# An FFT block with an ELU feed-forward layer on one core: prologue reordered, x rows moved to partition 0, scratch tensors padded, A units of batch 1 placed ahead of most Y units

## The chip, the cores and the metric

The kernel runs on one core of one Trainium2 chip. The metric is the device time of the whole program in microseconds (us). Besides the times there is one profiled execution with a trace of every instruction; its engines are named PE (matmuls), PEld (weight loads of PE), DVE, ACT, POOL and SP, and a trailing q (ACTq, SPq) marks an engine's issuing of DMAs. Times in the trace count from the start of the span.

## The reference, cut to what matters

```python
# x: (8, 3008, 256); w_r, w_i: (256, 256); w_in: (256, 2048); w_out: (2048, 256)
X = np.fft.rfft(x, axis=1)
Yr = Xr @ w_r - Xi @ w_i + b_r
Yi = Xr @ w_i + Xi @ w_r + b_i
Yr = np.sign(Yr) * np.maximum(np.abs(Yr) - 0.01, 0.0)      # Yi the same
y = np.fft.irfft(Yr + 1j * Yi, n=3008, axis=1)
h = y.reshape(-1, 256) @ w_in
g = np.where(h > 0.0, h, np.exp(np.minimum(h, 0.0)) - 1.0)
out = g @ w_out
```

A real FFT over the sequence, a complex linear layer with soft shrinkage, the inverse FFT, then a feed-forward layer of width 2048 with an ELU.

## The kernel before

The sequence of 3008 is split as 47 x 64 (N1 x N2), and both transforms are done as matmuls with matrices of sines that the kernel computes itself at its start. For each of the eight batches there are five kinds of units:

- **A** (`unit_A`, eight units per batch, two per chunk `ci` of x): the first step of the forward transform. Two f32 matmuls take a chunk of x from the tile `xts[ci]` with the matrix M1; the result is evicted to the tile A and stored in the scratch tensor DA in DRAM.
- **X** (`unit_X`, six): DA is read back in another order into the tile Z (`load_Z`), and eight matmuls with M2 give the spectrum XT.
- **M** (`unit_M`, twelve): the complex linear layer with bias and shrinkage (PE, then DVE, then two POOL operations).
- **B** (`unit_B`, six): the first step of the inverse transform with M3; the eviction goes to Bz and the result into the scratch tensor DB in DRAM.
- **Y** (`unit_Y`, eight): DB is read back as the tiles Bs (`load_Bs`, four), and matmuls with M4 give yT, the input of the feed-forward layer.

The feed-forward layer of a batch is a loop over 48 pairs (`PER`: six blocks of 512 tokens, eight pairs of feature tiles each). Each pair has a `front` (four matmuls, L582, then one or two ACT operations), an ELU on DVE and partly POOL (L602, L606, L617, L619; its result is gT) and, two pairs later, a `back` (eight matmuls, L639). `psH` has two buffers for what `front` writes, so that the front of pair i + 2 waits until the ELU of pair i has read its buffer. The units of the next batch are woven into this loop: `plan(b)` writes out for each pair which units run ahead of its front (`f0`) and which loads are issued behind it (`f1`). The single buffer of the pool `psF` serves one unit at a time. While batch 0 is in the feed-forward loop, `seq` begins with fourteen units: Y units 2 to 7 of batch 0, which is not yet fully transformed back, mixed with A units 0 to 7 of batch 1 (written "a"); after a7 the loads of Z of batch 1 are issued, and X unit 0 of batch 1 stands at pair 15. Behind them comes the list `mid`, which all batches share. It holds the six B units; at units 1, 3 and 5 the store of Bz to DB is issued from ACT (L246).

Batch 0 itself is transformed before the loop, in the **prologue**, with nothing to run beside it. Its parts in program order: 20 filler matmuls (`idle_pe`, on constant data, their result is not used); the loads of x, issued from POOL (`load_x`), each chunk as 80 + 14 rows that go to partitions 17 to 110 (P0 = 17) of tiles with 111 partitions; the zeroing of partitions 0 to 16, on ACT for chunks 0 and 1 (`zero_rows`, L314), on POOL for chunks 2 and 3 (L327); M1 from iotas and a sine; `phases(g)` on DVE (L385 to L394) and `sines(g, c)` on ACT (L401) for the three column groups g of M2; the A units with `alone=True`, whose stores are issued from SP (L133); the loads of Z; the transposes that give M4 and M3 (L451, L466); conversions of the weights (L474 to L477); the loads of the feed-forward weights; then X, M and B units of batch 0 and the stores of DB from SP (L241); the four loads of Bs, half from SP and half from ACT; filler matmuls while they come; Y units 0 and 1. A small POOL copy (`gate`) holds POOL until a given tile has landed, so that the x loads of batch 1 are issued only behind the first Bs.

Each engine executes its own instructions in program order, and the order is written by hand throughout. A DMA is issued by the engine named in the code and stands in that engine's order.

Of the kernel before, what the change touches and what calls it, by code (L numbers as in the profile page):

```python
# [8 lines left out]
ALU = mybir.AluOpType  # L9
# [12 lines left out]
NH = N2 // 2  # L22
P0 = N2 - N1
P1 = P0 + 2 * N1


@with_exitstack
def kernel(
# [66 lines left out]
    def load_x(b, ci):  # L95
        xv = x[b].rearrange("(r m c) d -> c r m d", c=4, m=8)
        for r0, r1 in ((0, 80), (80, 2 * N1)):
            nc.gpsimd.dma_start(xts[ci][P0 + r0 : P0 + r1], xv[ci, r0:r1].bitcast(F32R))

# [11 lines left out]
    def unit_A(b, u, alone=False, on_dve=False):  # L111
        ci, uu = u // 2, u % 2
        if uu == 0:
            if alone:
                A_of[b, ci] = wk4.tile([4 * K1, 8, D], BF16, name="A", tag="Bs")
            else:
                A_of[b, ci] = wk2.tile([4 * K1, 8, D], BF16, name="A", tag="A")
            if ci == 0:
                DA_of[b] = dram.tile([NH, 4 * K1, D], BF16, name="DA", tag="DA")
        xt, A = xts[ci], A_of[b, ci]  # L120
        dav = DA_of[b].rearrange("(m c) r d -> c r m d", c=4)
        ps = unit_ps("aps", alone)
        for j in range(2):
            nc.tensor.matmul(  # L124
                ps[0 : 4 * K1, j, :], lhsT=M1[:],
                rhs=xt[:, 4 * uu + 2 * j : 4 * uu + 2 * j + 2, :], start=True, stop=True,
            )
        evac(
            A[:, 4 * uu : 4 * uu + 4, :].rearrange("p n d -> p (n d)"),
            ps[0 : 4 * K1].rearrange("p a b -> p (a b)"), on_dve,  # L130
        )
        if alone:
            nc.sync.dma_start(dav[ci, :, 4 * uu : 4 * uu + 4, :], A[:, 4 * uu : 4 * uu + 4, :])  # L133
        elif uu == 1:
            nc.scalar.dma_start(dav[ci], A[:])
# [79 lines left out]
    def unit_B(b, v, alone=False, on_dve=False):  # L215
        if v % 2 == 0:
            Bz_of[b, v // 2] = wk2.tile([P, 8, D], BF16, name="Bz", tag="Bz")
            if v == 0:
                DB_of[b] = dram.tile([K1, P, D], BF16, name="DB", tag="DB")
        Bz, Y = Bz_of[b, v // 2], Y_of.pop((b, v))  # L220
        ps = unit_ps("bps", alone)
        for pp in range(2):
            for c in range(2):
                for s in range(2):
                    nc.tensor.matmul(  # L225
                        ps[:, s, pp * D : pp * D + D],
                        lhsT=M3[s * N2 : s * N2 + N2, 2 * v + pp, c, :],
                        rhs=Y[s * N2 : s * N2 + N2, pp, c * D : c * D + D],
                        start=(c == 0), stop=(c == 1),
                    )  # L230
        o = 4 * (v % 2)
        Bv = Bz[:, o : o + 4, :].rearrange("p (q s) d -> p s q d", s=2)
        psv = ps[:].rearrange("p s (q d) -> p s q d", d=D)
        if on_dve:
            nc.scalar.copy(Bv[:, 0], psv[:, 0])
            nc.vector.tensor_copy(Bv[:, 1], psv[:, 1])
        else:
            nc.scalar.copy(Bv, psv)  # L238
        if alone:
            k0 = 4 * v  # L240
            nc.sync.dma_start(  # L241
                DB_of[b][k0 : k0 + 4].rearrange("k p d -> p k d"), Bz[:, o : o + 4, :]
            )
        elif v % 2:
            k0 = 8 * (v // 2)
            nc.scalar.dma_start(DB_of[b][k0 : k0 + 8].rearrange("k p d -> p k d"), Bz[:])  # L246

    def load_Bs(b, w, engs=None):
        engs = engs or (nc.sync, nc.sync)
        Bs = wk4.tile([4 * K1, 8, D], BF16, name="Bs", tag="Bs")  # L250
        dv = DB_of[b].rearrange("k (c m) d -> (k c) m d", c=2)
        for h in range(2):
            n0 = h * NH + 8 * w
            engs[h].dma_start(Bs[h * 2 * K1 : h * 2 * K1 + 2 * K1], dv[:, n0 : n0 + 8, :])
        Bs_of[b, w] = Bs
# [32 lines left out]
    with tc.tile_pool(name="stagep", bufs=1) as stagep:  # L288
# [22 lines left out]

        def zero_rows(ci):
            for m in range(0, 8, 2):
                nc.scalar.activation(  # L314
                    xts[ci][0:P0, m : m + 2, :].rearrange("p n d -> p (n d)"), busy[0:P0, :],
                    AF.Copy, scale=0.0,
                )

        pcol = iota([P, 1], "pcol", [[0, 1]], cm=1)
# [4 lines left out]
        for ci in range(1, 4):  # L324
            load_x(0, ci)
        for ci in range(2, 4):
            nc.gpsimd.memset(xts[ci][0:P0].bitcast(F32), 0.0)  # L327
        ident = stagep.tile([P, P], F32, name="ident")
# [6 lines left out]
        def wrap(v, r):  # L335
# [4 lines left out]

        half = col("half", pcol, 0.5, ALU.mult, -0.5 * P0 - 0.25, ALU.add)
        halfm = col("halfm", half, CMAGIC, ALU.add)
# [7 lines left out]
        wrap(v1[:], r1t[:])  # L350
        zero_rows(0)
        nc.scalar.activation(r1t[:], v1[:], AF.Sin, bias=0.0, scale=SIN_SCALE)
        zero_rows(1)
        h1col = stagep.tile([P, 1], F32, name="h1col")
        nc.vector.scalar_tensor_tensor(
            h1col[:], n1col[:], -2.0, pcol[:], ALU.mult, ALU.add
        )
        h1col = col("h1m", h1col, float(-P0), ALU.add)
        isx = col("isx", pcol, P0 - 0.5, ALU.is_gt)
        h0col = stagep.tile([P, 1], F32, name="h0col")  # L360
        nc.vector.scalar_tensor_tensor(
            h0col[:], h1col[:], -1.0, isx[:], ALU.mult, ALU.add
        )
        nc.vector.tensor_tensor(h0col[:], h0col[:], isx[:], ALU.mult)
        nc.vector.tensor_tensor(h1col[:], h1col[:], isx[:], ALU.mult)
        ccol = col("ccol", pcol, N2 - 0.5, ALU.is_gt)
# [38 lines left out]

        for g in range(2):
            phases(g)
# [23 lines left out]
        unit_A(0, 3, alone=True)  # L431
        sines(1, 0)
        idle_pe(4)
        unit_A(0, 4, alone=True)
# [4 lines left out]
        unit_A(0, 6, alone=True)  # L439
        unit_A(0, 7, alone=True, on_dve=True)  # L440
        phases(2)
        sines(1, 1)
        dume = stagep.tile([P, 1], F32, name="dume")
        sines(2, 0)
        sines(2, 1)
        nc.scalar.activation(dume[:], pcol[:], AF.Exp, scale=0.0)
        for g in range(3):
            load_Z(0, 8 * g, 8 * g + 8, 0, NH, (nc.sync, nc.scalar))

# [5 lines left out]
        nc.vector.tensor_scalar(  # L455
            M4[:], m4ps[0 : 4 * K1, P0:P1], wcol[0 : 4 * K1, :], None, ALU.mult
        )
# [3 lines left out]
        for g in range(3):  # L461
# [8 lines left out]
            nc.vector.tensor_copy(M3[:, 4 * g : 4 * g + 4, :, :], m3ps[:])  # L470
            if g == 1:
                idle_pe(6)
        idle_pe(10)
        nc.vector.tensor_copy(wcat_r[:, :, 0:D], w_r_f[:])  # L474
# [68 lines left out]
    for q in range(4):  # L543
        nc.vector.tensor_scalar_mul(
            w_in_s[:, :, q * FQ : q * FQ + FQ], w_in_f[q][:], 2.0 / S
        )
    idle_pe(28)
    for u in range(2):
# [122 lines left out]
    def plan(b):  # L671
# [11 lines left out]
        if b == 0:  # L683
            lead, seq = 1, (
                [("y", 2), ("a", 0), ("a", 1), ("y", 3), ("a", 2), ("a", 3), ("y", 4), ("a", 4),
                 ("a", 5), ("y", 5), ("a", 6), ("a", 7), ("y", 6), ("y", 7)] + mid
            )
# [91 lines left out]
```

## Time and profile before

| what | value |
|---|---|
| median of 3 runs | 968.77 us (967.47 to 969.27) |
| profiled execution, whole time | 967.99 us |
| its span, from first to last instruction | 966.2 us |
| PE busy | 924.5 us |
| PE busy from 60.6 to 180 us | 111.72 of 119.40 us |
| PE busy from 295 to 410 us | 113.44 of 115.00 us |
| ACT busy from 295 to 410 us | 90.75 of 115.00 us |
| DB store issued from ACT (L246) | 21 times, 382 ns each |
| DB store issued from SP (L241) | 6 times, 360 ns each |
| DA store issued from ACT (L135) | 28 times, 328 ns each |

The share of busy time is an average over the prologue (some 60 us), the stretch in which batch 0 and batch 1 overlap (60 to 180 us), and six more stretches of about 115 us each, in the last of which nothing but the feed-forward layer is left. The page also shows the span in 40 equal slices:

```profile
PE   6969899999999999999999999999999999999997
PEclk9879999999999999999999999999999999999999
DMA  9996941856165543836246461665438102411011
```

Each digit is a slice of 24.2 us: the busy share in tenths for PE, the granted clock of PE in tenths, the busy share of the DMA engines. Slices 1 and 3 are the prologue's beginning and the stretch from 48 to 72 us.

### The profile page before, as it was taken

The page shows a single profiled execution, that of the slowest core. Times are in us where ns is not written, and L with a number is a line of the kernel's source. Part 1 is how long each engine was busy: PE and PEld are TensorE (multiplying, and loading weights), DVE is VectorE, ACT ScalarE, POOL GpSimd, SP SyncE. Part 2 cuts the span into 40 slices and gives each one's busy share as a digit, 9 for nine tenths or more (in the row PEclk, how much of TensorE's full clock was granted, in tenths as well). Part 3 has the DMA queues.
Part 4 walks back from the last instruction along what each step waited for, and adds up shares of the span by engine and source line. Part 5 has one row for each costly group of instructions (what it writes and reads, how often), then busy time and mean ns, then how long its engine had stood idle before and what let it go on. Part 6 is the DMA issues. An engine that isn't in the chain of part 4 may idle for free.

```text
span 966.2 us, 16677 instructions
## 1 busy us (share of the span) xinstructions
PE 924.5 (96%) x6398; PEld 655.5 (68%) x6502; DVE 733.9 (76%) x855; ACT 721.6 (75%) x819; POOL 281.1 (29%) x356
## 2 busy tenths in 40 slices
PE   6969899999999999999999999999999999999997
PEld 2436666777667766777667776776767777677775
DVE  8747666776788777887778777787778867888996
ACT  6538678888877788778886888877887787667664
POOL 5520343034302442115312243024421143321332
PEclk9879999999999999999999999999999999999999
DMA  9996941856165543836246461665438102411011
GB/s 215 271 191 109 185 90 45 217 107 129 45 185 128 87 76 83 220 56 115 71 133 161 74 119 55 179 136 87 76 82 212 33 22 66 110 45 42 22 44 42
DMA packets 113987, 105.43 MB, mean 109 GB/s; under 512 B 7794, under 2 KB 107636, under 8 KB 113012
## 3 DMA queue, kind: packets, MB, share of 16 engines
q1 hardware_dynamic: 41892, 54.02, 21.1%
q0 software_dynamic: 27680, 26.74, 19.8%
q10 hardware_dynamic: 44336, 23.60, 9.4%
q8 instruction: 51, 0.84, 0.4%
q14 instruction: 28, 0.23, 0.1%
HBM read 54.53 MB, written 49.81 MB: 108 GB/s over the span
## 4 chain that ended last, share of the span: by engine, by line
PE 57%; DVE 20%; ACT 12%; issue 4%; DMA 4%; POOL 1%; ACTq 1%; DVEq 0%; SPq 0%; another core or an unknown queue 0%; POOLq 0%
PE ps_o L639 21%; PE hps L582 21%; DVE gT L602 9%; PE mps L177 7%; DVE gT L606 4%; DVE Et L617 4%; ACT Et L592 3%; PE aps L124 2%; DVE Et L619 2%; ACT Et L589 2%; ACT A L109 2%; PE bps L225 2%; DMA xt<-in_x_dram 2%; PE xps L158 2%; ACT osb L651 2%
## 5 line engine op out<-in xcount | busy, mean ns | idle before, releaser
L639 PE MATMUL ps_o<-w_out_r,gT 128*128 128x256 f32 (+1 forms) x3072 | 491.9, 302 | 1.6 <-DVE gT L602 1.0
L639 PEld LDWEIGHTS ps_o<-w_out_r,gT 128*128 128x128 f32 (+1 forms) x3072 | 410.7, 187 | 67.6 <-DVE gT L602 12.9
L582 PE MATMUL hps<-yT,w_in_s 128*128 128x512 bf16 (+1 forms) x1465 | 386.4, 378 | 11.9 <-DVE gT L606 4.4
L592 ACT ACTIVATE Et<-hps 128x1024 f32<-128x1024 f32 (+1 forms) x300 | 302.0, 1007 | 102.1 <-PE hps L582 73.9
L602 DVE SCALAR_TENSOR_TENSOR gT<-Et,hps 128x1024 fp32r<-128x1024 f32 (+1 forms) x181 | 214.7, 1186 | 68.1 <-ACT Et L590 50.4
L606 DVE SCALAR_TENSOR_TENSOR gT<-hps,Et 128x1024 fp32r<-128x1024 f32 (+1 forms) x203 | 245.6, 1210 | 17.5 <-PE hps L582 0.5
L582 PEld LDWEIGHTS <-w_in_s 128*128 128x128 bf16 x1536 | 133.4, 98 | 152.2 <-issue 35.8
L619 DVE TENSOR_SCALAR Et<-Et 128x1024 f32<-128x1024 f32 (+1 forms) x203 | 139.0, 685 | 91.7 <-ACT Et L592 89.7
L192 POOL TENSOR_SCALAR clip<-yb 128x512 f32<-128x512 f32 x84 | 51.6, 614 | 313.1 <-DVE yb L184 258.8
L617 POOL TENSOR_SCALAR Et<-Et 128x512 f32<-128x512 f32 (+1 forms) x97 | 59.5, 613 | 274.3 <-ACT Et L592 274.3
L589 ACT ACTIVATE Et<-hps 128x1024 f32<-128x1024 f32 x84 | 86.4, 1029 | 69.9 <-PE hps L582 69.9
L193 POOL TENSOR_TENSOR Y<-yb,clip 128x512 bf16<-128x512 f32 x84 | 107.2, 1277 | 7.0
L184 DVE TENSOR_TENSOR yb<-mps,bias_bc 128x512 f32<-128x512 f32 x96 | 66.2, 690 | 32.9 <-PE mps L177 22.4
L590 ACT ACTIVATE Et<-Et 128x1024 f32<-128x1024 f32 x84 | 88.8, 1057 | 2.7
L109 ACT CAST A<-aps 96x1024 bf16<-96x1024 f32 x63 | 63.4, 1009 | 15.4 <-PE aps L124 14.9
L109 ACT CAST yT<-yps 128x752 bf16<-128x752 f32 x63 | 49.7, 788 | 18.8 <-PE yps L265 18.8
L177 PE MATMUL mps<-wcat_r,XT 128*128 128x512 bf16 x176 | 54.7, 384 | 0.6 <-ACT XT L165 0.2
L177 PE MATMUL mps<-wcat_s,XT 128*128 128x512 bf16 x177 | 53.9, 379 | 0.8
L617 DVE TENSOR_SCALAR Et<-Et 128x512 f32<-128x512 f32 (+1 forms) x97 | 54.2, 559 | 0.4 <-ACT Et L592 0.2
L168 ACT CAST XT<-xps 128x1024 bf16<-128x1024 f32 x46 | 45.9, 1000 | 10.4 <-PE xps L158 10.4
L177 PEld LDWEIGHTS <-XT 128*128 128x128 bf16 x384 | 30.7, 98 | 29.0 <-issue 1.1
L238 ACT CAST Bz<-bps 128x1024 bf16<-128x1024 f32 x47 | 47.3, 1008 | 3.6 <-PE bps L225 3.6
(95 smaller groups left out, 420.1 us busy)
## 6 DMA issues: line engine op xcount, KB each, us to landing
xt<-in_x_dram POOLq DMA_DIRECT2D x32, 640.0 KB, 6.2
out_dram<-osb SPq DMA_DIRECT2D x160, 128.0 KB
Bs<-DB SPq DMA_DIRECT2D x60, 192.0 KB
DA<-A ACTq DMA_DIRECT2D x28, 384.0 KB
DB<-Bz ACTq DMA_DIRECT2D x21, 512.0 KB
Z<-DA SPq DMA_DIRECT2D x28, 256.0 KB
Z<-DA SPq DMA_DIRECT2D x34, 128.0 KB
xt<-in_x_dram POOLq DMA_DIRECT2D x32, 112.0 KB, 5.8
```

Source lines behind the costliest of these rows:

```text
L109: nc.scalar.copy(dst, src)
L177: nc.tensor.matmul(ps, lhsT=XT[:, dt, c, o : o + P], rhs=wm[:, dt, :], start=(m == 0 and dt == 0), stop=(m == 1 and dt == 1),)
L193: nc.gpsimd.tensor_tensor(Y_of[b, q][:, i, :], yb[:], clip[:], ALU.subtract)
L582: nc.tensor.matmul(hps[:, s, 0:nb], lhsT=w_in_s[:, dt, ft * P : ft * P + P], rhs=yT[:, dt, bs : bs + nb], start=(dt == 0), stop=(dt == 1),)
L589: nc.scalar.activation(E_, hps[:, :, 0:nb], AF.Relu, scale=-1.0)
L590: nc.scalar.activation(E_, E_, AF.Exp, scale=-1.0)
L592: nc.scalar.activation(E_, hps[:, :, 0:nb], AF.Exp)
L602: nc.vector.scalar_tensor_tensor(gT[:, :, 0:nb], E_, -1.0, h_, ALU.add, ALU.max)
L606: nc.vector.scalar_tensor_tensor(gT[:, :, 0:nb], h_, 0.0, E_, ALU.max, ALU.add)
L617: eng.tensor_scalar(E_[:, s], E_[:, s], 1.0, 0.0, ALU.min, ALU.max)
L619: nc.vector.tensor_scalar(E_, E_, 1.0, -1.0, ALU.min, ALU.add)
L639: nc.tensor.matmul(po[q][0 : t1 - t0, i_ % 2, :], lhsT=gT[:, s, t0:t1], rhs=w_out_r[:, ft, :], start=(ft == 0 and i_ % 2 == 0), stop=(ft = ...
```

## The change

- x rows start at partition 0: P0 is gone, P1 is 94, M1 and the tiles of x have 94 partitions, and neither `zero_rows` nor the POOL memsets are left. The columns that chose rows of M1 by partition (`isx`, `h1m`) are simpler.
- The scratch tensors are padded: DA has 98 rows of 256 for each of its 32 indices instead of 96; DB is laid out as 48 rows of 66 x 256 instead of 24 of 128 x 256. So a store of Bz is two DMAs, one for partitions 0 to 63 and one for 64 to 127, instead of one. This holds for the six stores of the prologue (SP) and for the three per batch later (ACT).
- In the prologue, `phases(2)` follows `phases(1)` directly; `sines(1, 1)` comes ahead of A unit 4; A unit 7 is evicted by ACT instead of DVE; Z is loaded in two parts (k 0 to 7, and 8 to 23) instead of three, and the dummy Exp comes behind the issues of these loads; the fillers among and behind the transposes are 12 at one place instead of 6 and 10 at two; those before Y unit 0 are 34 instead of 28.
- In the plan of batch 0 the eight A units of batch 1 stand in a row behind Y units 2 and 3, and Y units 4 to 7 behind them.

```diff
-P0 = N2 - N1
-P1 = P0 + 2 * N1
+P1 = 2 * N1
+RA = 4 * K1 + 2
+RB = N2 + 2
...
-            nc.gpsimd.dma_start(xts[ci][P0 + r0 : P0 + r1], xv[ci, r0:r1].bitcast(F32R))
+            nc.gpsimd.dma_start(xts[ci][r0:r1], xv[ci, r0:r1].bitcast(F32R))
...
-                DA_of[b] = dram.tile([NH, 4 * K1, D], BF16, name="DA", tag="DA")
+                DA_of[b] = dram.tile([NH, RA, D], BF16, name="DA", tag="DA")
...
-        dav = DA_of[b].rearrange("(m c) r d -> c r m d", c=4)
+        dav = DA_of[b][:, 0 : 4 * K1, :].rearrange("(m c) r d -> c r m d", c=4)
...
-                DB_of[b] = dram.tile([K1, P, D], BF16, name="DB", tag="DB")
+                DB_of[b] = dram.tile([2 * K1, RB, D], BF16, name="DB", tag="DB")
...
-        if alone:
-            k0 = 4 * v
-            nc.sync.dma_start(
-                DB_of[b][k0 : k0 + 4].rearrange("k p d -> p k d"), Bz[:, o : o + 4, :]
-            )
-        elif v % 2:
-            k0 = 8 * (v // 2)
-            nc.scalar.dma_start(DB_of[b][k0 : k0 + 8].rearrange("k p d -> p k d"), Bz[:])
+        if alone or v % 2:
+            nk = 4 if alone else 8
+            k0 = 4 * v + 4 - nk
+            src = Bz[:, o : o + 4, :] if alone else Bz[:]
+            dst = DB_of[b].rearrange("(k c) n d -> c n k d", c=2)
+            for c in range(2):
+                (nc.sync if alone else nc.scalar).dma_start(
+                    dst[c, 0:N2, k0 : k0 + nk, :], src[c * N2 : c * N2 + N2]
+                )
...
-        dv = DB_of[b].rearrange("k (c m) d -> (k c) m d", c=2)
...
-            engs[h].dma_start(Bs[h * 2 * K1 : h * 2 * K1 + 2 * K1], dv[:, n0 : n0 + 8, :])
+            engs[h].dma_start(Bs[h * 2 * K1 : h * 2 * K1 + 2 * K1], DB_of[b][:, n0 : n0 + 8, :])
...
-        for ci in range(2, 4):
-            nc.gpsimd.memset(xts[ci][0:P0].bitcast(F32), 0.0)
...
-        zero_rows(0)
         nc.scalar.activation(r1t[:], v1[:], AF.Sin, bias=0.0, scale=SIN_SCALE)
-        zero_rows(1)
...
-        for g in range(2):
+        for g in range(3):
             phases(g)
...
         sines(1, 0)
+        sines(1, 1)
         idle_pe(4)
         unit_A(0, 4, alone=True)
...
-        unit_A(0, 7, alone=True, on_dve=True)
-        phases(2)
-        sines(1, 1)
-        dume = stagep.tile([P, 1], F32, name="dume")
+        unit_A(0, 7, alone=True)
         sines(2, 0)
         sines(2, 1)
+        for k0, k1 in ((0, 8), (8, K1)):
+            load_Z(0, k0, k1, 0, NH, (nc.sync, nc.scalar))
+        dume = stagep.tile([P, 1], F32, name="dume")
         nc.scalar.activation(dume[:], pcol[:], AF.Exp, scale=0.0)
-        for g in range(3):
-            load_Z(0, 8 * g, 8 * g + 8, 0, NH, (nc.sync, nc.scalar))
...
-            if g == 1:
-                idle_pe(6)
-        idle_pe(10)
+        idle_pe(12)
...
-    idle_pe(28)
+    idle_pe(34)
...
-                [("y", 2), ("a", 0), ("a", 1), ("y", 3), ("a", 2), ("a", 3), ("y", 4), ("a", 4),
-                 ("a", 5), ("y", 5), ("a", 6), ("a", 7), ("y", 6), ("y", 7)] + mid
+                [("y", 2), ("y", 3)] + [("a", u) for u in range(8)]
+                + [("y", u) for u in range(4, 8)] + mid
```

More of the change, by code (lines that the diff above doesn't have):

```diff
@@ L310, in flat @@
             return t.rearrange("p a b -> p (a b)")
[L312 to L317, printed above, removed]
         pcol = iota([P, 1], "pcol", [[0, 1]], cm=1)
@@ L338, in wrap @@
             nc.vector.tensor_tensor(v, r, v, ALU.add)
-        half = col("half", pcol, 0.5, ALU.mult, -0.5 * P0 - 0.25, ALU.add)
+        half = col("half", pcol, 0.5, ALU.mult, -0.25, ALU.add)
         halfm = col("halfm", half, CMAGIC, ALU.add)
@@ L357 @@
         )
[L358 to L365, printed above, removed]
+        h0col = col("h0col", h1col, -1.0, ALU.mult, 1.0, ALU.add)
         ccol = col("ccol", pcol, N2 - 0.5, ALU.is_gt)
@@ L455 @@
         nc.vector.tensor_scalar(
-            M4[:], m4ps[0 : 4 * K1, P0:P1], wcol[0 : 4 * K1, :], None, ALU.mult
+            M4[:], m4ps[0 : 4 * K1, 0:P1], wcol[0 : 4 * K1, :], None, ALU.mult
         )
```

## The prediction

> **What bounds it now.** I read the busy totals first. PE works 96% of the span and its waits after 108 us add up to about 8 us, so past that point every microsecond taken from PE or added to it counts. What is loose lies ahead of 108 us, so next I read the chain of waits there.
>
> ```profile
> PE 924.5 (96%) x6398; PEld 655.5 (68%) x6502; DVE 733.9 (76%) x855; ACT 721.6 (75%) x819; POOL 281.1 (29%) x356
> ```
>
> ```profile
> 8.75 10.07 DMA xt<-in_x_dram
> ...
> 20.13 1.22 DVE A L107
> 21.35 0.46 DVE v L385
> ...
> 29.71 2.16 PE ips L281 x10
> 31.86 0.46 PE xps L158 x8
> ...
> 55.12 3.97 DMA Bs<-DB
> ...
> 60.15 7.50 DMA xt<-in_x_dram
> ...
> 67.78 1.14 PE aps L124 x2
> ...
> 100.43 3.08 DMA Z<-DA
> ```
>
> To be seen: the start hangs on the x load (until 18.8), then on the late group of phases on DVE, then on PE's own filler matmuls. X unit 0 starts at 31.86 because the fillers end there, not because its Z came then. Later PE waits for Bs, for batch 1's x, and for batch 1's Z. What these waits cost, and at which clock, the PE timeline and the stretches tell:
>
> ```profile
> 67.78 1.14 PE L124 MATMUL aps<-xt,M 111*96 111x512 f32 x2 [2.55 <-DMA xt<-in_x_dram]
> 103.64 0.61 PE L158 MATMUL xps<-M,Z 128*128 128x128 bf16 x8 [2.45 <-DMA Z<-DA]
> 62.00:77.00 15.00, 12.23 (x59) 7.32 (x58) 6.88 (x8) 7.93 (x9) 2.81 (x5) 0.61 1.97 214
> 104.50:108.00 3.50, 3.48 (x19) 3.02 (x19) 1.26 (x2) 1.82 (x2) 0.00 (x0) 0.51 0.71 148
> ```
>
> The number after POOL's column is the granted clock: 0.61 and 0.51 where other stretches have 1.00. So each wait is paid twice, once idle and once at half speed. The trace's clock records put the half clock at 22.6 to 29.5, 60.2 to 73.8 and 104.5 to 108.0 us.
>
> **Prologue.** Phases of group 2 move from after A unit 7 (21.3 to 25.1 on DVE) to after group 1. There DVE sat idle (17.4 to 20.1), and without the two POOL memsets the first operation of group 1 should take the 0.53 us that it takes at 21.27 instead of 2.84. So group 2 is done near 18.5. The 16 zeroing operations on ACT (L314, 8 x 0.61) and the memsets (2 x 1.83) go; both lay under the x load, worth nothing by themselves. A unit 7's eviction moves to ACT behind unit 6's: 20.68 + 1.01 = 21.7 against 21.35 on DVE, so its DA store and the Z loads start 0.35 later. Sines of group 2 follow at 21.7 to 23.0, the transposes end near 23.6, twelve fillers at 0.216 end near 26.2. Now Z binds. SP issued it at 24.41, ACT only at 25.38, behind the last sine; now both go at about 24.8. In the packet records SP's Z begins 1.2 us after its issue, ACT's 1.7 us, and ACT's first third takes 2.2 us; a load is seen about 0.9 us after its last packet (the gate at 32.08 against 31.16). X0: 24.8 + 1.7 + 2.2 + 0.9 = 29.6. But the last two thirds are now one load, and X2 needs all of it. 1.57 MB at the 221 GB/s of the stretch 25 to 32 takes 7.1 us, at the 346 of 44 to 48 us 4.5; from 26.0, plus 0.9, X2 starts at 31.4 to 34.0. It started at 34.13. I take the middle, 32.6: **-1.5 us**, between 0 and -2.7. The dummy Exp moves behind the Z issues: its table load (1.28) is hidden until X0's eviction near 30.
>
> x rows from partition 0: the load runs at 214 GB/s (4 to 16 us). The uneven halves that this gives have a near row in Bs, mostly below partition 64, at 256 GB/s (57 to 59 us): above 214, so no loss is taken; the source is read as before, so no gain. I allow 0.5 us each way. A matmuls with 94 rows instead of 111 stream the same 512 columns: nothing.
>
> **DB and Bs of batch 0.** The last store becomes two issues on SP, 0.36 each (L241): **+0.4** on the way to Bs. The padding may speed the 3.97 us of Bs: a pitch of 33 KB for 32, of 49 for 48. Nearest rows: 256 GB/s against 346 elsewhere, so the move part (about 2.3 us) could shrink by 0.6; or not. Taken: -0.4. Together **0**, from -0.6 to +0.4. Fillers 28 to 34: 6 x 0.216 = 1.3 us more. They ended at 57.2 with Y0 at 59.13, so they still end before Bs and only shorten the idle stretch ahead of the half clock.
>
> The Trainium skill (DMA: Bandwidth & Descriptors, "Rules for kernel authors") speaks against the split: two transfers to disjoint partition halves serialize, so use one. Here it costs one issue per store by our rows, with or without it. The same page ("Latency and other measured facts") says that a pad of +192 B on a huge pitch changed nothing and +4 KiB did; 1 KB lies between.
>
> **Batch 0: A units ahead of Y.** Batch 1's A0 moves from pair 2 to pair 3, with Y3 before it. Batch 1's x then arrives while front 2 and back 0 run. Before, A0 at 67.78 was followed by front 2 (1.73), back 0 (1.71), A1 (0.86) and front 3 at 73.0; now by front 3 after one A unit, 0.5 us: 4.7 us less. If the clock still falls to half before, only the 1.8 us of front 2 and back 0 at full speed are won. PE is busy some 57% of the 7 us before A0 (Y0 to Y3, three fronts, one back) against 37% of the 3.4 us before the fall at 60.2 us. So full clock is likelier, but eight A units in a row have a trap: A chunk 2 takes the buffer of chunk 0, whose store lands about 2 us after x is in, and A4 is now earlier: about 1 us. 0.65 x 3.7 + 0.35 x 1.8: **-3.1**, from -1.8 to -4.7.
>
> A7 comes at pair 10 instead of 12, X0 stays at 15. The chain A7, DA store, Z took 103.64 - 93.97 = 9.7 us; with the osb copies ahead of A7's eviction (1.05) 10.6. Five pairs give 2.3 + 4 x 2.15 = 10.9. So the 2.45 us wait goes, and with it 3.4 us at half clock (1.7): 4.1. With 0.4 kept for the thin margin: **-3.7**, from -2.4 to -4.2. The Trainium skill (TensorE: Matmul & The Clock Gate, "Part 1") says that the clock drops after an idle window of about 3.4 us. The row speaks against that as a bound: 2.45 us of waiting were enough here; by the page only 2.45 would be won.
>
> **Steady state: two DB stores for one.** This is the price. In each of seven batches ACT issues three more DMAs:
>
> ```profile
> 250.12 0.61 PE L225 MATMUL bps<-Y,M 64*128 64x256 bf16 x8
> 252.33 0.38 ACTq L246 DMA_DIRECT2D DB<-Bz  x1
> 252.81 1.02 ACT L592 ACTIVATE Et<-hps 128x1024 f32<-128x1024 f32 x1 [0.51 <-DVE gT L602]
> 255.94 1.02 PE L582 MATMUL hps<-yT,w_in_s 128*128 128x512 bf16 x4 [0.26 <-DVE gT L606]
> 269.80 1.02 ACT L592 ACTIVATE Et<-hps 128x1024 f32<-128x1024 f32 x1 [0.50 <-ACT Bz L238]
> ```
>
> Behind the issue stands an Exp; behind it DVE's gT, and PE needs that for the front two pairs later. At the second store PE already waits 0.26, so another 0.37 is lost in full. At the first, gT ends 0.10 before PE comes: 0.27. At the third PE comes just as gT ends, but ACT has 0.30 to spare one A unit later: I take 0.15. 7 x (0.27 + 0.37 + 0.15) = **+5.5**. Bounds: only the second store pays, 7 x 0.37 = 2.6; all pay in full, 21 x 0.37 = 7.8.
>
> **Sum.** -1.5 + 0 - 3.1 - 3.7 + 5.5 = -2.8. The profiled execution took 967.99, its span 966.2; that is 0.8 under the median of 968.77. From the median: **966.0 us**. All terms at their best: -2.7 - 0.6 - 0.5 - 4.7 - 4.2 + 2.6 = -10.1; at their worst 0 + 0.4 + 0.5 - 1.8 - 2.4 + 7.8 = +4.5.
>
> **Rivals.**
> 1. ACT hides the second issue: it idles some 24 of 115 us per batch. Against it: those idle stretches do not lie behind the stores. Then -8.3 with 0 in place of 5.5: 960.5.
> 2. The reorder saves idle time but not the clock, PE being fed as thinly before A0: -1.5 - 1.8 - 2.4 + 5.5 = -0.2, 968.6. For it: PE's duty there stays near one half.
> 3. Slower: the second issue on ACT's queue at all 21 stores. Half stores of 64 partitions read one half of SBUF's partitions and could hold the next DA store and the A buffer up; one such wait of 0.44 exists, at 281.06. At 0.37 + 0.15 each, 21 x 0.52 = 10.9, against -8.3: +2.6, 971.4. It decides from 0.40 us per store on, since 21 x 0.40 = 8.3. For it: PE has no slack there. Against it: 0.10 and 0.30 of slack were seen.
> 4. The change does not remove the Z wait, the margin being 0.3 us. Then 2.4 of the 3.7 is given back: 968.4.
>
> **How the numbers follow.** Forecast 0.42, rival 1 0.18, rival 2 0.11, rival 3 0.22, rival 4 0.07. A measurement of this kernel tells about 0.2% (1.9 us) from no change. Faster than 966.8: most of the forecast (0.33) and rival 1, 0.51. Within: 0.08 of the forecast, rivals 2 and 4, and 0.01 of rival 3: 0.27. Slower than 970.7: 0.22. The forecast's own range is 962 to 969; that of 8 in 10 reaches into rivals 1 and 3: 959.5 to 972.5.
>
> **What would show it.** X0 near 29.6 and X2 near 32.6; the clock at 1.00 from 60 to 74 us and at 104 to 108; no wait of PE for Z near X0 of batch 1. Two issues of DB at each site in the steady part, the next Exp 0.9 instead of 0.5 us after the Bz eviction, and PE waits for gT near 0.6 behind the second store. A batch then takes about 115.8 us instead of 115.0. It is wrong if batches stay as long as before (rival 1), or if they grow by over 1.2 us (rival 3: 8.3 / 7).

## The result and the profile after

The changed kernel takes 982.28 us (980.55 to 983.88) where the kernel before takes 968.88 (967.47 to 969.27): a ratio of 1.0141, 95% interval 1.012 to 1.0161. The prediction was 966.0, from 959.5 to 972.5: it had the sign wrong.

The page of the changed kernel begins with the busy time of each engine and its share of the span:

```profile
span 978.8 us, 16690 instructions
PE 922.1 (94%) x6400; PEld 655.3 (67%) x6504; DVE 730.8 (75%) x850; ACT 716.2 (73%) x811; POOL 276.6 (28%) x354
```

PE does 2.4 us less work than before (924.5), and the span is 12.6 us longer: PE idles 15.0 us more. So the first question is where it waits. These are PE's waits after 108 us, where before little was loose; first the kernel before, then the changed one. The columns are what waited, for what, us in total, times, longest.

```profile
PE hps L582 <- DVE gT L606: 4.0, 12, 0.9
...
PE aps L124 <- ACT A L109: 0.5, 3, 0.2
```

```profile
PE hps L562 <- DVE gT L586: 9.8, 24, 1.8
PE mps L178 <- ACT yT L110: 4.2, 6, 0.9
PE mps L178 <- DVE yb L185: 4.1, 8, 1.4
PE aps L125 <- ACT A L110: 2.4, 6, 1.2
```

(Line numbers differ: the front is L582 before and L562 after, the operation that makes gT L606 and L586, the A matmul L124 and L125.) The wait of the fronts for gT, for which the prediction had a price, grew by 5.8 us. Three others, which it did not have, grew from 0.5 to 10.7: M units that wait for the eviction of yT or for yb, A units that wait for the eviction of the A unit before. These all pass through the single buffer of `psF`.

Measured from the first feature matmul of one batch to that of the next, batches 1 to 6 took 110.8 to 113.3 us before and 113.0 to 116.0 after; together they are 13.0 us longer. Batch 0 went from 129.7 to 126.1, and the loop starts 3.1 us later (64.1 against 61.0). So in these two executions the new order helped, the prologue did not, and both are small beside the steady part. (The batches of the kernel before take 113.1 us on average; the 115.0 that the prediction names is the length of the stretch it had looked at, and nothing in its sum hangs on it.)

What happens there is seen at a DB store. ACT's timeline around two of them, start and length first, idle time before in brackets:

```profile
229.74 1.01 ACT L239 CAST Bz<-bps 128x1024 bf16<-128x1024 f32 x1
230.79 1.28 ACTq L246 DMA_DIRECT2D DB<-Bz  x2
232.18 1.02 ACT L572 ACTIVATE Et<-hps 128x1024 f32<-128x1024 f32 x1 [1.42 <-DVE gT L586]
...
252.33 1.30 ACTq L246 DMA_DIRECT2D DB<-Bz  x2
253.74 1.03 ACT L572 ACTIVATE Et<-hps 128x1024 f32<-128x1024 f32 x1 [1.43 <-PE yps L266]
254.66 0.78 ACT L110 CAST yT<-yps 128x752 bf16<-128x752 f32 x1
```

The two issues take 1.28 us, where one took 0.38, and the next Exp comes 1.42 us after the eviction, where it came after 0.5. (The releaser named in the bracket is misleading: ACT waits for nothing but its own queue.) PE, a little later:

```profile
255.49 0.59 PE L178 MATMUL mps<-wcat_r,XT 128*128 128x512 bf16 x2 [0.68 <-ACT yT L110]
...
256.87 1.02 PE L562 MATMUL hps<-yT,w_in_s 128*128 128x512 bf16 x4 [0.36 <-DVE gT L586]
```

The yT eviction stands behind the late Exp, the M unit waits for the buffer that it frees (0.68), and then the front for its gT (0.36). That is 1.04 us lost at one store. The issues of the changed kernel, on ACT and (in the prologue) on SP, as minimum, median and maximum in ns:

```profile
L246 ACTq DMA_DIRECT2D DB<-Bz x42: 582/628/1541, 134.7 to 846.9; - x42
L246 SPq DMA_DIRECT2D DB<-Bz x12: 574/608/708, 44.3 to 55.7; - x12
```

The store of half the partitions takes longer to issue than the store of all of them: 0.63 against the 0.38 us of before (366 to 390 ns).

### The profile page after: what moved, and what is told of

It reads as the page before. It is cut to its first block, busy times and chain, and to the rows that moved or that the text cites. A ratio compares the mean times of both kernels' runs of the same rounds, so it can differ in the third digit from the quotient of the medians.

```text
span 978.8 us, 16690 instructions
## 1 busy us (share of the span) xinstructions
PE 922.1 (94%) x6400; PEld 655.3 (67%) x6504; DVE 730.8 (75%) x850; ACT 716.2 (73%) x811; POOL 276.6 (28%) x354
## 4 chain that ended last, share of the span: by engine, by line
PE 45%; DVE 23%; ACT 15%; issue 5%; DMA 4%; ACTq 3%; POOL 1%; DVEq 0%; another core or an unknown queue 0%; POOLq 0%
PE hps L562 17%; PE ps_o L619 16%; DVE gT L582 10%; PE mps L178 6%; ACT Et L572 6%; DVE gT L586 5%; DVE Et L597 4%; DVE Et L599 2%; ACTq L246 2%; ACT A L110 2%; ACT Et L569 2%; ACT Bz L239 2%; DMA DA<-A 2%; PE aps L125 2%; PE xps L159 1%
## 5 line engine op out<-in xcount | busy, mean ns | idle before, releaser
L619 PEld LDWEIGHTS ps_o<-w_out_r,gT 128*128 128x128 f32 (+1 forms) x3072 | 410.0, 187 | 64.4 <-DVE gT L582 12.4
L562 PE MATMUL hps<-yT,w_in_s 128*128 128x512 bf16 (+1 forms) x1465 | 383.4, 375 | 18.4 <-DVE gT L586 11.4
L582 DVE SCALAR_TENSOR_TENSOR gT<-Et,hps 128x1024 fp32r<-128x1024 f32 (+1 forms) x181 | 214.7, 1186 | 67.8 <-ACT Et L570 50.1
L586 DVE SCALAR_TENSOR_TENSOR gT<-hps,Et 128x1024 fp32r<-128x1024 f32 (+1 forms) x203 | 245.6, 1210 | 17.1 <-DVE Et L599 0.5
L562 PEld LDWEIGHTS <-w_in_s 128*128 128x128 bf16 x1536 | 132.2, 97 | 158.2 <-issue 38.2
L125 PE MATMUL aps<-xt,M 94*96 94x512 f32 x128 | 41.4, 410 | 10.4 <-DMA xt<-in_x_dram 6.3
```

Of the source, the lines that this page charges most:

```text
L562: nc.tensor.matmul(hps[:, s, 0:nb], lhsT=w_in_s[:, dt, ft * P : ft * P + P], rhs=yT[:, dt, bs : bs + nb], start=(dt == 0), stop=(dt == 1),)
L582: nc.vector.scalar_tensor_tensor(gT[:, :, 0:nb], E_, -1.0, h_, ALU.add, ALU.max)
L586: nc.vector.scalar_tensor_tensor(gT[:, :, 0:nb], h_, 0.0, E_, ALU.max, ALU.add)
L619: nc.tensor.matmul(po[q][0 : t1 - t0, i_ % 2, :], lhsT=gT[:, s, t0:t1], rhs=w_out_r[:, ft, :], start=(ft == 0 and i_ % 2 == 0), stop=(ft = ...
```

## The experiments

The theory: the loss is the time that the two issues hold ACT's order, three times per batch. The rivals: the transfers themselves, the padded layout, the new prologue.

**One part undone or done alone.** The kernels were measured in three groups, each with the kernel before beside them. It took 968.38 us (965.54 to 969.92), 967.67 (965.53 to 971.65) and 967.97 (964.53 to 970.25). The ratios below are to the kernel before of the same group.

*The changed kernel with one unpadded DB store.*

```diff
-        if alone or v % 2:
-            ...
-            for c in range(2):
-                (nc.sync if alone else nc.scalar).dma_start(
-                    dst[c, 0:N2, k0 : k0 + nk, :], src[c * N2 : c * N2 + N2]
-                )
+        if alone:
+            nc.sync.dma_start(
+                DB_of[b][k0 : k0 + 4].rearrange("k p d -> p k d"), Bz[:, o : o + 4, :]
+            )
+        elif v % 2:
+            nc.scalar.dma_start(DB_of[b][k0 : k0 + 8].rearrange("k p d -> p k d"), Bz[:])
```

> The changed kernel with DB and its stores as before (24 x 128 x 256, one DMA per store); all else of the change stays. Theory: the loss in the steady part is ACT's time for two issues of some 0.63 us where there was one of 0.38. Then the issue returns to 0.38, the six steady batches (115.02 to 116.02 us from front to front, 113.02 the last) return to 112.9 to 113.3 and 110.8, and the time falls from 982.3 by 13 to 16 us to 966 to 969. Rival: the batches grew through something else of the change (A tiles of 94 partitions, DA padded). Then they stay near 115 us and the time stays above 978.

Measured: 963.58 us (961.45 to 965.76), ratio 0.9955, interval 0.9941 to 0.9969; batches 1 to 5 take 112.9 to 113.3 us. Against the changed kernel that is 18.7 us: the DB store is all of the loss and more, and what remains of the change is a gain of some 5 us. (The fall is larger than the 13 to 16 us expected. The two profiled executions lie 14.8 us apart, 980.55 and 965.76, of which batches 1 to 6 are 13.9.)

*The kernel before with nothing but the padded, halved DB store.*

```diff
-                DB_of[b] = dram.tile([K1, P, D], BF16, name="DB", tag="DB")
+                DB_of[b] = dram.tile([2 * K1, RB, D], BF16, name="DB", tag="DB")
...
+            for c in range(2):
+                (nc.sync if alone else nc.scalar).dma_start(
+                    dst[c, 0:N2, k0 : k0 + nk, :], src[c * N2 : c * N2 + N2]
+                )
```

> The kernel before with nothing but the padded DB and its two stores of 64 partitions. Theory: the split alone is the whole price. Six steady batches grow from 113 to about 115, batch 0's own three stores cost about 2, DB to Bs in the prologue up to 1: the time rises from 968.4 by 14 to 19 us to 982 to 987. Rival: a good part of the price comes only together with the rest of the change; then it rises by less than 10.

Measured: 985.19 us (984.76 to 985.87), ratio 1.0176, interval 1.0153 to 1.02: +17.5 us, the same from the other side. PE's waits after 108 us are of the same four kinds as in the changed kernel: 7.8 us for gT in fronts, 3.9 for yT, 3.9 for yb and 2.8 for A.

*The changed kernel without the padding of DB.*

```diff
-RB = N2 + 2
+RB = N2
```

> The changed kernel with two stores of 64 partitions but DB without padding (48 rows of 64 x 256). It tells why one issue takes 0.63 us. If the pitch makes it, an issue falls to about 0.38, the excess per store from 0.9 to 0.4, and the time falls by some 7 us to about 975. If the shape (64 partitions) makes it, issues stay at 0.6 to 0.65 and the time stays within 2 us of 982.

Measured: 982.79 us (981.91 to 983.55), ratio 1.0157, interval 1.014 to 1.0174, the issues 582/630/1614 ns: nothing changed. The issue is not long because of the pitch in DRAM; the rival of the layout falls, and so does any gain from it.

*The kernel before with nothing but the new order of batch 0.*

```diff
-                [("y", 2), ("a", 0), ("a", 1), ("y", 3), ("a", 2), ("a", 3), ("y", 4), ("a", 4),
-                 ("a", 5), ("y", 5), ("a", 6), ("a", 7), ("y", 6), ("y", 7)] + mid
+                [("y", 2), ("y", 3)] + [("a", u) for u in range(8)]
+                + [("y", u) for u in range(4, 8)] + mid
```

> The kernel before with nothing but the new order of batch 0 (Y2, Y3, A0 to A7, Y4 to Y7). Theory: the order alone removes the wait for Z and most of the half clock, worth 5 to 7 us: 962 to 964. Rival: the A row on ACT with its DA stores takes most of it back, and the time stays within 2 us of 968.9; PE would then wait for ACT's A evictions near pairs 6 to 8.

Measured: 961.98 us (961.71 to 963.65), ratio 0.9946, interval 0.9929 to 0.9964: -6.4 us. The longest of PE's waits from 60 to 108 us in this kernel:

```profile
PE aps L124 <- ACT A L109: 2.3, 1, 2.3
```

The waits for batch 1's x (2.55) and Z (2.45) are gone. In their place stands this one of 2.3 for an A unit's eviction: the A buffer that the prediction called a trap, since chunk 2 needs the buffer of chunk 0, whose store has to land first. ACT's eviction of A unit 4 shows it:

```profile
81.98 1.01 ACT L109 CAST A<-aps 96x1024 bf16<-96x1024 f32 x1 [3.05 <-DMA DA<-A]
```

The prediction put this trap at about 1 us. Behind the wait the granted clock is at half from 82.8 to 86.2 us. Nine of the kernels measured here have the new order. In five of them (this one, three others with the changed prologue and the stores on ACT, and the changed kernel with its half stores on SP) the wait is 2.3 to 2.8 us, and a stretch of half clock of 3.4 us follows. In the other four, the changed kernel among them, it is 1.0 to 1.8 us and none follows.

**Is it ACT's queue or the transfers?** *The changed kernel with the two half stores issued from SP.*

```diff
-                (nc.sync if alone else nc.scalar).dma_start(
+                nc.sync.dma_start(
```

> The changed kernel with the two stores issued from SP in the steady part too. Theory: the loss is ACT's time, as Exp stands behind the issues; SP has nothing of the sort behind it. Issues keep their 0.6 us, the steady batches return to about 113, and the time falls from 982.3 to 962 to 967. Rival: the half stores hurt by their transfers (Bs or DA come later); then the batches stay above 114 and the time above 975.

Measured: 960.93 us (959.26 to 962.11), ratio 0.9924, interval 0.9898 to 0.995. PE's waits after 108 us:

```profile
PE aps L125 <- ACT A L110: 0.8, 5, 0.2
PE hps L562 <- DVE gT L586: 0.8, 3, 0.3
```

The same two transfers per store, with the same shapes, and the waits for gT fall from 9.8 to 0.8; those of the M units for yT and yb are gone from the list. On SP the issues are as long as on ACT:

```profile
L246 SPq DMA_DIRECT2D DB<-Bz x54: 574/626/1492, 44.4 to 829.6; - x54
```

They stand in nobody's way there. So the halved transfer costs nothing that can be seen; its issue in ACT's order costs everything. The time is a little below the 962 to 967 us expected, because even the one store of the kernel before was not free: batches 1 to 5 now take 112.6 us on average where they took 113.1.

**Two issues of the length that the prediction took.** If the mechanism was right and only the length wrong, two issues of 0.37 us should cost the 5.5 us of the prediction. Two kernels try it, both the kernel before with each ACT store cut in two, all 128 partitions in each: by k 0 to 3 and 4 to 7, or by even and odd k.

```diff
-            nc.scalar.dma_start(DB_of[b][k0 : k0 + 8].rearrange("k p d -> p k d"), Bz[:])
+            for k in (0, 4):
+                nc.scalar.dma_start(
+                    DB_of[b][k0 + k : k0 + k + 4].rearrange("k p d -> p k d"), Bz[:, k : k + 4, :]
+                )
```

> The kernel before with each DB store of ACT cut into two in the other direction: 128 partitions with 4 of the 8 k each. This is the price that the prediction had in mind: the row of SP's stores of this shape says 0.36 per issue. If the issue's length is what the prediction got wrong and not the slack behind it, issues take 0.36 to 0.38, the next Exp comes 0.4 later, and the time rises by 5.5 us (2.6 to 7.8) to about 974. If any second issue costs 0.6, it rises by 14 or more, as with the halves. If ACT has more slack than seen, by less than 2.6.

Measured: 968.24 us (963.87 to 970.89), ratio 0.9996, interval 0.9977 to 1.0016: no cost. But ACT's timeline shows that this kernel does not test the price:

```profile
231.04 0.38 ACTq L247 DMA_DIRECT2D DB<-Bz  x1
231.09 1.01 ACT L238 CAST Bz<-bps 128x1024 bf16<-128x1024 f32 x1
232.14 0.38 ACTq L247 DMA_DIRECT2D DB<-Bz  x1
232.90 1.02 ACT L595 ACTIVATE Et<-hps 128x1024 f32<-128x1024 f32 x1 [0.79 <-ACT Bz L238]
```

k 0 to 3 were evicted by an earlier unit. Their store is issued from 231.04 to 231.42, beside the last eviction (231.09 to 232.10), and only one issue is left behind it. Here the Exp comes 0.79 us behind the eviction; over all 21 stores the median is 0.50, where the kernel before has 0.51. (What the expectation shared out between the theories is thus not decided by this kernel.) With even and odd k both stores need the last eviction:

```diff
+            for h in range(2):
+                nc.scalar.dma_start(
+                    DB_of[b][k0 + h : k0 + 8 : 2].rearrange("k p d -> p k d"), Bz[:, h : 8 : 2, :]
+                )
```

> The kernel before, with each steady DB store cut into two of 128 partitions that take every second k; both need the last eviction of Bz, so two issues stand one behind the other ahead of the next Exp. The cut into k 0-3 and k 4-7 cost nothing, but there the first issue lay beside the last eviction. Theory 1 (the length of the issue is what counts, and the price worked out in the prediction holds for issues of 0.37 us): 21 x 0.37 us of issue shift the Exp by 0.4 us, from 0.5 to 0.9 us behind the eviction; batches of 113.9 us where the kernel before has 113.1, the kernel 971 to 976 us. Rival (0.4 us of late Exp is hidden, the price sets in above it): batches 113.1, the kernel within 1.5 us of the one before, at 968, though the Exp is 0.4 us later. Rival 2 (two stores in place of one cost by themselves, whatever the issue takes): about 985 us, as with the two halves of partitions.

Measured: 974.79 us (971.73 to 976.05) beside 967.97 for the kernel before; ratio 1.0065, interval 1.0046 to 1.0085: +6.8 us. Of the theories it is the first that holds: the time lies in its range, but the issues are longer than it took them, and the Exp comes 1.07 us behind the eviction instead of 0.9. ACT's timeline and PE's waits after 108 us:

```profile
232.65 0.94 ACTq L247 DMA_DIRECT2D DB<-Bz  x2
233.69 1.02 ACT L595 ACTIVATE Et<-hps 128x1024 f32<-128x1024 f32 x1 [1.07 <-issue]
```

```profile
PE hps L585 <- DVE gT L609: 9.9, 24, 1.5
PE mps L177 <- ACT yT L109: 1.8, 6, 0.3
PE mps L177 <- DVE yb L184: 0.6, 1, 0.6
PE aps L124 <- ACT A L109: 0.6, 1, 0.6
```

The waits for gT grow by 5.9 us, those through `psF` only from 0.5 to 3.0. The pair of issues takes 0.94 us here, more than twice 0.38: the first takes 0.37 to 0.39, the second 0.52 (median). Between this kernel and the halves of 64 partitions lie 0.34 us per store, and they open the second path:

| issue between eviction and Exp | time of it | waits for gT | waits through psF | batches 1 to 5, mean |
|---|---|---|---|---|
| none, two halves on SP | 0 | 0.8 | 0.8 | 112.6 us |
| one (before) | 0.38 us | 4.0 | 0.5 | 113.1 us |
| two, even and odd k | 0.94 us | 9.9 | 3.0 | 114.2 us |
| two, halves of 64 partitions (changed) | 1.28 us | 9.8 | 10.7 | 115.3 us |

(The first and last rows are the changed kernel, the other two the one before; with one store the changed kernel's batches take 113.0, so the steady part may be compared across them.) Divided by three stores per batch and taken before rounding, the first 0.38 us cost 0.18 each, the next 0.56 cost 0.35, the last 0.34 cost 0.36: at the start half of it is hidden, at the end all of it is paid.

**The prologue.** *The changed kernel with x rows at partition 17 again, and all that belongs to them.*

```diff
-P1 = 2 * N1
+P0 = N2 - N1
+P1 = P0 + 2 * N1
...
+        zero_rows(0)
         nc.scalar.activation(r1t[:], v1[:], AF.Sin, bias=0.0, scale=SIN_SCALE)
+        zero_rows(1)
```

> The changed kernel with the rows of x from partition 17 again, zeroed rows included. Theory: rows from partition 0 slow the load of x (A unit 6 started at 20.37 instead of 18.96). Then A6 starts near 19.0 and what follows in the prologue comes 1 to 1.5 us earlier; the time falls by 1 to 2.5 us (x of batch 1 is waited for too). Rival: the x load differs from execution to execution, and A6 stays near 20.4 with the time within 1 us.

Measured: 981.49 us (979.07 to 982.09), ratio 1.0136, interval 1.0113 to 1.0158, the same as the changed kernel. From A unit 0 to A unit 6 the traces show 10.7 to 11.5 us with the rows at 17 (seven kernels, mean 11.1) and 11.2 to 12.0 at 0 (six kernels, mean 11.7). So the load may be half a us slower at 0; the ranges overlap, and the time does not tell it.

*The kernel with one DB store (the first experiment) and Z of batch 0 in three loads.*

```diff
-        for k0, k1 in ((0, 8), (8, K1)):
+        for k0, k1 in ((0, 8), (8, 16), (16, K1)):
```

> The changed kernel with DB as before and Z of batch 0 in three loads. Theory: X2 waits for Z because k 8 to 23 come as one load (X0 at 30.1, X2 at 35.8 with DB as before), and the half clock at 35 to 39 follows from that. Then X2 comes about 2.5 us after X0, near 32.6, front 0 comes 1.5 to 3 us earlier, and the time falls from 963.6 to 960.5 to 962. Rival: the loads of w_in, which now start at 29, hold Z up however it is cut; then X2 stays past 34.5 and the time within 1 us of 963.6.

Measured: 962.34 us (959.05 to 963.18), ratio 0.9944, interval 0.9921 to 0.9966. X unit 2 of the changed kernel on PE, and then of this one:

```profile
35.05 0.61 PE L159 MATMUL xps<-M,Z 128*128 128x128 bf16 x8 [2.39 <-DMA Z<-DA]
```

```profile
32.60 0.61 PE L159 MATMUL xps<-M,Z 128*128 128x128 bf16 x8
```

With the second third as a load of its own, X2 starts at 32.60 in place of 35.05 and no half clock follows. The feature loop starts at 59.0 us. In six kernels with the prologue of before (one of them with the halved stores) it starts at 61.0 to 63.2, in five with the changed one and Z in two loads at 62.0 to 64.6. Against the first experiment (64.4) that should bring some 5 us, but the medians differ by 1.2 only. The profiled executions are no typical ones here: the one of the first experiment, 965.76, is the slowest of its ten, the one of this kernel, 959.05, the fastest of its five. Between these two the trace accounts for all of the 6.7 us: 5.4 by the start of the loop, 2.6 by batch 0, and batches 1 to 6 take 1.3 more (676.7 and 675.4). So a single trace tells where time went in one execution; what three loads of Z are worth on average, the medians put at 1.2 us, and the two intervals overlap.

**What beats both.** Two kernels with the steady DB store issued from SP, as one DMA of 128 partitions: the last kernel above (changed prologue with Z in three, new order), and the kernel before with the new order alone.

```diff
-            nc.scalar.dma_start(DB_of[b][k0 : k0 + 8].rearrange("k p d -> p k d"), Bz[:])
+            nc.sync.dma_start(DB_of[b][k0 : k0 + 8].rearrange("k p d -> p k d"), Bz[:])
```

> The changed kernel with one unpadded DB store, Z of batch 0 in three loads, and the steady DB stores issued from SP in place of ACT. Theory (even the one issue of 0.38 us stands in ACT's order between the eviction of Bz and the next Exp): the next Exp comes straight behind the eviction, batches of 112.5 us in place of 112.9, over seven batches 3 us less than with the store on ACT (962.3): 957 to 960 us. Rival (the store waits on SP behind other transfers, so DB is later and Bs with it; or 0.38 us was hidden): 961 to 964 us, the same as with the store on ACT.

Measured: 955.32 us (954.43 to 957.71), ratio 0.9875, interval 0.9855 to 0.9895. It is 7.0 us under the same kernel with its store on ACT, twice what was expected. That kernel comes from another group of runs; the two profiled executions, 959.05 and 955.07, differ by 4.0, and batches 1 to 6, 676.7 and 672.5 us, explain all of that. So 4 us are shown for the store, and the other 3 are not. PE's fronts wait 1.0 us for the gT of L586 after 108 us in the whole kernel.

> The kernel before with nothing but the new order of batch 0 and the steady DB stores on SP. Theory (both gains add up: -6.4 us by the order as measured, -3 us by the seven batches): 958 to 960.5 us, as fast as the changed prologue with the same stores, since that prologue gave 1 to 2 us at most. Rival (the prologue's part is worth what its front at 58.8 us showed, some 2 us): this one is 2 us or more behind the kernel with the changed prologue and Z in three loads.

Measured: 958.38 us (956.4 to 959.87), ratio 0.9899, interval 0.9881 to 0.9917. Both gains add up, as the theory had it: against the new order alone the store on SP gives 3.6 us. But the changed prologue with Z in three loads is worth 3.1 us beside it in the medians (the loop starts at 59.4 against 61.0 us), which is what the rival said, though the two intervals overlap a little. With the store on ACT the same comparison shows no gain of the prologue: 962.34 us against 961.98 for the new order alone. So its worth is open between nothing and 3 us.

Not tried: the padding of DA by itself, and the new numbers of fillers against the old ones.

## Why the prediction was wrong

**What bounds the kernel** was read rightly: past 108 us PE has no slack, and a few tenths of a us on ACT reach it 21 times.

**The step that failed** is the term "steady state: two DB stores for one", +5.5 with bounds of 2.6 and 7.8. It measured +17.5 with the halved stores alone. Two things in it were wrong, and the experiments part them:

- *The length of an issue.* The prediction wrote "so another 0.37 is lost in full" and bounded the whole with "21 x 0.37". The 0.37 came from the rows of the store as it was, 128 partitions (0.38 on ACT, 0.36 on SP). The edit changes the shape of the store, and the halves take 0.63 each: the pair 1.28 instead of 0.75. So the upper bound was no bound: it bounded where the delay falls, not how long it is. Put the measured length into the same working, where each store loses the delay less a slack of 0.10, 0 and 0.22 us: the halves delay the Exp by 0.90 us, which gives 7 x (0.80 + 0.90 + 0.68) = 16.7, near the 17.5. So the length of the issue is the bulk of the miss. With two issues of 128 partitions +6.8 was measured (4.5 to 8.2 by the interval) against 5.5; but there the delay was 0.56, not 0.37, for which the same working gives 9.5, so that this nearness is partly luck.
- *The path by which it reaches PE.* Only "DVE's gT, and PE needs that for the front two pairs later" was followed. That this wait grew by 5.8 us in the changed kernel, close to the 5.5, is chance: with even and odd k it grew by 5.9 at a shorter delay. Beyond that the loss shows up elsewhere: on ACT the evictions of Y and A units stand behind the same Exp, on DVE yb stands behind the same gT, and the single `psF` buffer waits for them. At 0.94 us this gives 2.5 us more of waiting, at 1.28 us 10.2. It is a path with more slack, and the longer issue used it up.

**Rival 3** named the right place, ACT's queue at all 21 stores, and the right sign; its price of 0.52 per store was worked out with the same 0.37, and 17.5 / 21 = 0.83 was measured. Its point of decision, 0.40 per store, was passed by far. The reason that it gave beside the issue, half stores that hold the A buffer up, is not what was seen: with the halves on SP the wait of A units for A is 0.8 us in all. Rival 1 (the second issue is hidden) falls: issues past the first are paid with 0.35 per store and more. The rule that two transfers to disjoint halves serialize, from the Trainium skill (DMA: Bandwidth & Descriptors, "Rules for kernel authors"), gave the right advice; but on SP the same two halves cost nothing that can be seen, so here it was the issue and not the transfer that made it right.

**The order of batch 0** was forecast at -3.1 - 3.7 = -6.8 and measured -6.4. In the changed kernel its parts came as written:

```profile
60.00:74.00 14.00, 9.19 (x73) 5.74 (x71) 6.63 (x7) 6.98 (x8) 5.55 (x9) 1.00 1.59 225
...
100.00:108.00 8.00, 7.89 (x60) 5.91 (x60) 7.03 (x9) 5.69 (x6) 1.44 (x3) 1.00 0.60 138
```

These are stretches of that kernel: length, then the busy time of PE, PEld, DVE, ACT and POOL, then the granted clock, 1.00 in both where it was 0.61 and 0.51. So rival 4 falls: no kernel with the new order waits for Z there. Rival 2 (the clock stays at half) falls for this execution, not for all. Alone, on the old prologue, the order still had a clock of 0.88 from 60 to 74 us, and in five of nine kernels a new half clock stands behind the wait for the A buffer, which the prediction had put at 1 us; that its sum came out right is partly luck. Its reading that each wait is paid twice was also too simple for the wait of 2.55 us: the half clock of the kernel before began at 60.2 us, five us ahead of that wait. (Small slips change nothing: the zeroing operations on ACT are 8 and not 16, 0.65 x 3.7 + 0.35 x 1.8 is 3.0, and 9.7 + 1.05 is 10.7, which leaves a margin of 0.2 us for Z.)

**The prologue**, forecast at -1.5 with X2 at 32.6 and a range to 34.0, went the other way. X0 came at 30.07 instead of 29.6. X2 came at 35.05, after a wait of 2.39, and the granted clock then fell to 0.52 from 36.0 to 39.5 us. The prediction had seen that X2 needs the whole second load and took the middle between two rates; the chain of waits shows the slow one, and the issues of Z began at 25.7 instead of 24.8 us:

```profile
27.10 7.71 DMA Z<-DA
```

The half clock behind this new wait was not in the sum, though the same text had priced it at two other waits of 2.5 us. (The Trainium skill's idle window of about 3.4 us, TensorE: Matmul & The Clock Gate, "Part 1", is no safe bound here either: 2.39 us of waiting were followed by half clock.) But it does not always follow. Five kernels have this prologue with Z in two loads; four of them, with waits of 2.17 to 3.17 us for X2, fall to half clock, and the fifth, the one without the padding, keeps the full clock after a wait of 2.81. The stretch from 36 to 39.5 us, first of the changed kernel, then of that one:

```profile
36.00:39.50 3.50, 3.28 (x18) 2.00 (x18) 0.81 (x2) 2.33 (x3) 3.33 (x4) 0.52 1.16 379
```

```profile
36.00:39.50 3.50, 3.45 (x34) 2.17 (x32) 2.88 (x4) 2.63 (x4) 3.32 (x4) 1.00 1.27 369
```

The loop of that kernel starts at 62.0 us, those of the four others at 64.1 to 64.6. What decides between the two was not found. In the changed kernel's profiled execution the loop started 3.1 us later than before; against the order alone the first experiment, which has this prologue too, is 1.6 us slower in the median, and the two intervals overlap.

**DB and Bs of batch 0**, forecast at 0: Bs took 3.79 us where it took 3.97, and the SP issues 0.61 instead of 0.36. The starts of the loop scatter by more than this between executions, so the term can't be checked closer than 1 to 2 us. No gain of the padding was found.

**Sum.** With what was measured, -6.4 + 17.5 + 1.6 = +12.7, against +13.4 for the whole change.

## What to carry to other kernels

When an edit changes the shape of a DMA, the length of its issue is an unknown cost and not the row of the old shape; ask which engine's order it stands in before asking what the transfer costs, and give it to an engine with room (here SP: -3.6 us for moving one store that was there already, with 7.0 between the medians of the other pair of kernels). A delay on an engine is to be followed to everything that stands behind it in its order, and down each path to the slack at its end: the first path gave the price of the first half us, another took over beyond it. And a wait of 2 to 3 us on PE is to be priced together with the half clock that may stand behind it, also where the change makes a new one: in these traces it followed most of such waits for Z and for the A buffer, not all.

## What was not expected of the hardware

- Issuing a store of 64 partitions takes 0.63 us on ACT and 0.61 to 0.63 on SP, of 128 partitions 0.38 on ACT and 0.36 to 0.39 on SP, of 96 partitions (the A store, on ACT) 0.32. It is so with a padded and an unpadded pitch, with 4 and with 8 blocks of k, on either engine. What makes it so was not found.
- Two issues of 128 partitions one behind the other took 0.94 us, 0.18 more than twice one; the second took 0.52. A single issue beside a running ACT operation took 0.38. The first of two halves took 0.60 in the median, the second 0.65, so that the halves are long from the first issue on.
